# Attention products moved one slot pair earlier, with key and query loads in three pieces each

## The chip, the cores and the metric

The kernel runs on one core of a Trainium2 chip. The metric is the device time of one execution in microseconds (us). The core's engines work side by side, each through its own list of instructions in order: TensorE (PE; its weight loads are shown apart as PEld), VectorE (DVE), ScalarE (ACT), GpSimd (POOL) and SyncE (SP). POOL and SP, and at two places ACT, also issue DMA transfers, which run on 16 shared DMA engines. An engine that has to wait for a semaphore holds up everything behind it in its list.

## What is computed

Attention with a threshold, then a two-layer feed-forward stage. Batch 8, 8 heads, 576 positions, head size 64; the feed-forward stage has 4608 tokens, width 512 and inner width 2048.

```python
def _attn_ref(q, k, v, tau) -> np.ndarray:
    scale = 1.0 / np.sqrt(q.shape[-1])
    scores = scale * np.matmul(q, k.transpose(0, 1, 3, 2))
    thresh = np.max(scores, axis=-1, keepdims=True) - tau
    scores = np.where(scores >= thresh, scores, -1000000000.0)
    scores = scores - np.max(scores, axis=-1, keepdims=True)
    attn = np.exp(scores)
    attn = attn / (np.sum(attn, axis=-1, keepdims=True) + 1e-09)
    return np.matmul(attn, v).astype(np.float32)

def _moe_ref(x, w_in, w_out) -> np.ndarray:
    h = x @ w_in
    relu6 = np.clip(h + 3.0, 0.0, 6.0)
    g = h * relu6 / 6.0
    return (g @ w_out).astype(np.float32)
```

The attention output of all heads, laid side by side, is `x`.

## The kernel before

The schedule is written out by hand (`manual_schedule`), as a list of 144 **slots**, 18 for each batch. A slot is 128 query rows of one pair of heads (a slot of type `t = 4` holds the last 64 rows of two pairs). Within a batch, slots 0 to 3 hold the first 256 queries of head pairs 0 and 1, slots 4 to 7 those of pairs 2 and 3, slots 8 and 9 the last 64 queries of all, slots 10 to 17 queries 256 to 511 in the same order. In this text "slot 6 of a batch" counts from the batch's first slot, and "slot 24" alone counts from the start.

What a slot goes through, and on which engine:

- **Scores** (PE, line 216). `burst(n + 2)`, at the end of every even slot n, computes the scores of slots n + 2 and n + 3 in float32, straight into PSUM. In its middle stands a relay, an empty instruction on POOL (line 205), for which the last matmuls wait; it stands behind POOL's normalising in that slot.
- **Maximum** (DVE, line 230), which also copies the scores to SBUF, and the **bias** from it (POOL, line 239).
- **Mask and exponential** (ACT, lines 244 and 249), with the row sum; its **reciprocal** (DVE, line 252).
- **Normalising** to bf16 (POOL, line 257), in the slot after.
- **Transpose** of the probabilities. For the first ten slots PE does it; for the other 134, SP issues a DMA transpose (line 268) into `pT` (or `pR` for the last 64 queries).
- **Attention product** (`av`, PE, line 286), ten matmuls for a pair of heads and a chunk of 256 queries (forty small ones for the last 64 queries). The table `products` says in which slot each stands; it reads the values `v` of the whole batch and the transposes of two slots. For pair 0 these are the chunk's first and third slot, for pair 2 its fifth and seventh (slots 4 and 6 of the first chunk, 14 and 16 of the second), so pairs 0 and 2 have their last probabilities later, measured from the product, than pairs 1 and 3.

A finished chunk gives eight items to `todo1`, the last 64 queries of two batches give four. From slot 14 on every slot takes one item, if there is one, and multiplies it with `w_in` (`mm1`, line 309 through a helper); the gate follows on ACT or DVE (lines 327, 329, 342). Finished items give parts to `todo2`; from slot 21 on each odd slot takes two of them and multiplies with `w_out` (`mm2_part`, line 309). Each output tile is scaled on DVE (line 361) and stored by SP (line 376). The items of the last 64 queries are transposed through SP (line 344, `g<-go`). Per batch there are 18 items, 18 parts and 9 products for 18 slots, so in the middle of the run every slot is full. What is left after slot 143 is worked off in the tail: first what stands in `todo1` and `todo2`, then the last attention products, then their items and parts.

A **quad** is four heads of a batch (quad 2b and 2b + 1). Its keys and queries are loaded as one tile each (`load`, line 86, tiles `nk` and `nq`, 576 KB, two buffers each) and put in order by 32x32 block transposes on DVE (`transpose_k`, line 110, in two parts of two instructions; `transpose_q`, line 96, in two parts), which are the `jobs` of given slots. The values of a batch come in eight pieces of 64 or 80 KB (line 119) into one of two buffers. All these issues stand at the end of their slot: on SP for the loads of batches 0 and 1, on POOL for the later ones and for the values and weights. DMA issues on POOL are part of its one list: the next bias and the next normalising wait behind them.

In each slot from 14 on, the order is: maximum of the next slot, reciprocal, attention product, first-product item with its gate, two second-product parts (odd slots), exponentials, masks, block transposes, normalising of the slot before, burst (even slots), output stores, DMA issues.

Of the kernel before, what the change touches and what calls it, by code (L numbers as in the profile page):

```python
# [20 lines left out]
def kernel(  # L21
# [10 lines left out]
    nc = tc.nc  # L32
# [6 lines left out]
    NSLOT = 18  # L39
# [33 lines left out]
    issues = {}  # L73
    jobs = {}

    def at(when, n, job):
        when.setdefault(n, []).append(job)
# [3 lines left out]
    def load(quad, of, t0=0, t1=T, by=nc.sync):  # L81
        b, g = divmod(quad, 2)
        if (quad, of) not in nat:
            nat[quad, of] = nat_pool.tile([P, T * D], F32, tag=("nq", "nk")[of], name=("nq", "nk")[of])
        src = (q, k)[of][b, 4 * g:4 * g + 4].rearrange("h (r t) d -> (h r) (t d)", r=R)
        by.dma_start(out=nat[quad, of][:, t0 * D:t1 * D], in_=src[:, t0 * D:t1 * D])
# [7 lines left out]
    def transpose_q(quad, t0, t1):  # L94
        rows = nat[quad, 0][:].rearrange("p (t j w) -> p t j w", j=2, w=32)
        nc.vector.transpose(out=qk_of(quad)[0][:].rearrange("p j (t w) -> p t j w", w=32)[:, t0:t1],  # L96
                            in_=rows[:, t0:t1])
# [3 lines left out]
    def transpose_k(quad, part):  # L101
        first, e = ((0, 5), (10, 4))[part]
        rows = nat[quad, 1][:].rearrange("p (t j w) -> p j t w", j=2, w=32)
        outs = qk_of(quad)[1]
        for j in range(2):
            for_u = rows[:, j, first:first + 2 * e].rearrange("p (u e) w -> p u e w", u=2)
            base = outs[:, j, :]
            o = base[:, 64 * part:64 * part + 64].rearrange("p (u w) -> p u w", u=2)
            o = bass.AP(tensor=o.tensor, offset=o.offset, ap=[list(o.ap[0]), [32, 2], [128, e], [1, 32]])
            last = nc.vector.transpose(out=o, in_=for_u)  # L110
        return last
# [3 lines left out]
    def load_v(b):  # L115
        def piece(a, g):
            t0, count = (((0, 5), (5, 5), (10, 4), (14, 4)), ((10, 4), (14, 4), (0, 5), (5, 5)))[a][g]
            c0 = 0 if a == 0 else 5 - count
            nc.gpsimd.dma_start(  # L119
                out=vsb[b % 2][32 * g:32 * g + 32].rearrange("p (hp a) c -> p a hp c", a=2)[  # L120
                    :, a, :, c0 * D:(c0 + count) * D],
                in_=v[b].rearrange("(hp a) (r t) d -> a r hp (t d)", a=2, t=T)[a][:, :, t0 * D:(t0 + count) * D])

        return [lambda a=a, g=g: piece(a, g) for g in range(4) for a in range(2)]
# [9 lines left out]
    def load_w_in(i):  # L134
        f0 = 512 * i
        nc.gpsimd.dma_start(out=w_in_sb[:, :, f0:f0 + 512],
                            in_=moe_w_in.rearrange("(ki p) f -> p ki f", p=P)[:, :, f0:f0 + 512])
# [252 lines left out]
    products = {}  # L390
    for b in range(B):
        n0 = b * NSLOT
        for hp in range(NPAIR):
            at(products, n0 + (6 if b == 0 else 8) + 2 * hp, (b, hp, 0))
            at(products, n0 + 18 + 2 * hp, (b, hp, 1))
        at(products, n0 + (14 if b == 0 else 16), (b, None, None))

    def multiply(n):
        copies = []
# [14 lines left out]
    for quad in range(2, 2 * B):  # L414
        b, g = divmod(quad, 2)
        n0 = (b - 1) * NSLOT
        when = (((1, 4), (7, 9))[g] if b == 1 else ((-1, 5), (7, 9))[g])
        for n, of in zip(when, (1, 0)):
            at(issues, n0 + n, lambda quad=quad, of=of: load(quad, of, by=nc.sync if quad < 4 else nc.gpsimd))
        when = (((4, 8, 10, 22), (12, 14, 18, 24)) if b == 1 else ((8, 10, 12, 20), (14, 16, 18, 22)))[g]  # L420
        for n, job in zip(when, (lambda quad=quad: transpose_k(quad, 0), lambda quad=quad: transpose_k(quad, 1),
                                 lambda quad=quad: transpose_q(quad, 0, 8), lambda quad=quad: transpose_q(quad, 8, T))):
            at(jobs, n0 + n, job)
# [4 lines left out]
    def v_pieces(b, slots):  # L428
        pieces = []

        def piece(i):
            if not pieces:
                pieces.extend(load_v(b))
            pieces[i]()

        for i, n in enumerate(slots):
            at(issues, n, lambda i=i: piece(i))

    v_pieces(0, (-1, -1, -1, -1, 0, 0, 0, 0))
    for b in range(1, B):  # L440
        v_pieces(b, (13, 14, 15, 16, 17, 18, 19, 20) if b == 1 else [(b - 1) * NSLOT + n for n in range(8, 24, 2)])
    for i, n in enumerate((0, 2, 2, 3)):
        at(issues, n, lambda i=i: load_w_in(i))
    for i, n in enumerate((4, 6, 8, 10)):
        at(issues, n, lambda i=i: load_w_out(i))
# [218 lines left out]
```

## Time and profile before

| what | value |
|---|---|
| device time, median of the runs | 501.76 us (lowest 500.86) |
| profiled execution: device time | 501.7 us |
| profiled execution: span on the core | 499.9 us |
| DVE scores maximum, L230 | 288 at 750 ns |
| ACT exponential, L249 | 288 at 671 ns |
| POOL normalising, L257 | 288 at 745 ns |
| POOL issue of a key or query load, L86 | 24 at 588 to 596 ns |
| key load, POOL issue to landing, 576 KB | 4.9 us (median) |
| query load, the same | 5.1 us |
| value piece, 80 KB / 64 KB | 4.3 / 3.4 us |
| DMA transpose of probabilities, issue to landing | 4.5 us |
| all DMA | 79.98 MB, 192770 packets |

Durations, idle times and landings come from one profiled execution; the device time contains the span and 1.8 us around it. In a row of a group or of the timeline, the shape to the right of the arrow is what is read, the number after "x" the count, and the bracket at the end tells how long the engine stood idle before and whose work ended that. In the rows of the stretches, the numbers in round brackets are counts of instructions.

### The profile page before, as it was taken

What the parts mean: (1) busy time and instruction counts of PE and PEld (TensorE: products, weight loads), DVE (VectorE), ACT (ScalarE), POOL (GpSimd) and SP (SyncE); (2) the same over time, 40 slices, a digit from 0 to 9 for tenths busy, and PEclk for the clock granted to TensorE, in tenths of its full rate; (3) what the DMA queues carried; (4) which work ended last, traced back from release to release, by engine and by line L of the source; (5) the groups of instructions that cost most, each with busy time, mean ns of one, the idle gap of its engine ahead of it and who ended that gap; (6) DMA issues with size and microseconds to landing.
All of it is one profiled execution on the core that took longest, in us unless ns stands there. A gap on an engine that the chain in (4) does not pass through costs nothing.

```text
span 499.9 us, 17390 instructions
## 1 busy us (share of the span) xinstructions
PE 484.7 (97%) x6797; PEld 359.5 (72%) x6802; DVE 445.8 (89%) x1154; ACT 441.6 (88%) x949; POOL 294.1 (59%) x537
## 2 busy tenths in 40 slices
PE   8888998999999999999999999999999999999996
PEld 7766765777777776777777776777777776777474
DVE  6999986999999999999999999999999999887243
ACT  3999997999999999999999999999999999999231
POOL 3786784666666666666666666766666565554000
PEclk9999998999999999999999999999999999999999
DMA  7999998997999887997999997998999878766421
GB/s 207 150 252 178 148 181 141 180 163 117 178 178 217 130 186 149 227 158 151 156 209 181 152 168 146 220 176 147 160 187 207 151 129 130 134 123 134 92 65 42
DMA packets 192770, 79.98 MB, mean 160 GB/s; under 512 B 171184, under 2 KB 183984, under 8 KB 192688
## 3 DMA queue, kind: packets, MB, share of 16 engines
q1 hardware_dynamic: 175456, 55.34, 65.0%
q0 software_dynamic: 16896, 23.07, 23.9%
q8 instruction: 53, 0.87, 0.7%
q10 hardware_dynamic: 336, 0.46, 0.3%
q14 instruction: 29, 0.24, 0.2%
HBM read 36.70 MB, written 9.44 MB: 92 GB/s over the span
## 4 chain that ended last, share of the span: by engine, by line
PE 82%; DVE 7%; issue 1%; ACT 1%; DMA 0%; SPq 0%; DVEq 0%
PE ps L309 48%; PE ps L216 27%; PE ps L286 7%; DVE s L230 4%; DVE g L342 1%; ACT r L327 1%; DVE osb L361 1%; DMA out_dram<-osb 0%; DVE kT L110 0%; DVE r L329 0%; DVE xT L294 0%; DVE pR L279 0%; SPq L376 0%; DVE qT L96 0%; DVE rinv L252 0%
## 5 line engine op out<-in xcount | busy, mean ns | idle before, releaser
L230 DVE TENSOR_SCALAR_CACHE_REDUCE s<-ps 128x576 f32<-128x576 f32 x288 | 205.0, 750 | 17.9 <-PE ps L216 15.2
L257 POOL TENSOR_SCALAR pn<-s,rinv 128x576 bf16<-128x576 f32 x288 | 210.8, 745 | 14.9 <-issue 1.3
L244 ACT ACTIVATE s<-s,bias 128x576 f32<-128x576 f32 x288 | 205.7, 762 | 8.3 <-POOL bias L239 8.3
L249 ACT ACTIVATE s<-s 128x576 f32<-128x576 f32 x288 | 192.3, 671 | 0.0
L216 PE MATMUL ps<-kT,qT 32*128 32x128 f32 (+3 forms) x2560 | 168.6, 418 | 6.5 <-DVE s L230 4.0
L216 PEld LDWEIGHTS ps<-kT,qT 32*128 32x128 f32 (+1 forms) x2560 | 125.1, 175 | 50.9 <-DVE s L230 11.5
L309 PE MATMUL ps<-xT,w_in_sb 128*64 128x256 bf16 (+1 forms) x1936 | 133.4, 275 | 0.5 <-DVE xT L294 0.5
L309 PE MATMUL ps<-w_out_sb,g 128*64 128x512 bf16 (+1 forms) x1020 | 130.8, 379 | 0.2
L309 PEld LDWEIGHTS <-w_in_sb 128*64 128x64 bf16 (+1 forms) x1936 | 106.0, 109 | 10.9 <-issue 3.3
L239 POOL TENSOR_SCALAR bias<-m 128x2 f32<-128x2 f32 (+1 forms) x147 | 27.6, 188 | 140.1 <-DVE rinv L252 125.9
L342 DVE SCALAR_TENSOR_TENSOR g<-r,ps 128x512 bf16<-128x512 f32 x128 | 87.4, 684 | 12.2 <-ACT r L327 8.5
L309 PEld LDWEIGHTS <-g 128*64 128x64 bf16 (+1 forms) x1024 | 61.6, 109 | 47.9 <-issue 0.2
L327 ACT ACTIVATE r<-ps,three 128x512 f32<-128x512 f32 x81 | 55.2, 686 | 22.8 <-PE ps L309 21.8
L249 ACT ACTIVATION_READ_ACCUMULATOR s<-s 128x1 f32 x288 | 54.6, 190 | 0.0
L286 PEld LDWEIGHTS <-v 128*64 128x64 bf16 x960 | 41.4, 111 | 15.8 <-issue 3.8
L286 PE MATMUL ps<-pT,v 128*64 128x256 bf16 x640 | 45.4, 273 | 1.3 <-DVE s L230 1.2
L329 DVE TENSOR_SCALAR r<-ps 128x512 f32<-128x512 f32 x63 | 43.3, 688 | 0.7 <-PE ps L309 0.4
L119 POOL DMA_DIRECT2D v<-in_v_dram x64 | 36.9, 578 | 10.1 <-DVE kT L110 4.7
L361 DVE TENSOR_SCALAR osb<-ps 128x512 f32<-128x512 f32 x32 | 21.9, 684 | 9.0 <-DMA out_dram<-osb 6.3
L110 DVE STREAM_TRANSPOSE kT<-nk 128x320 f32<-128x320 f32 (+1 forms) x64 | 26.3, 452 | 0.8 <-DMA nk<-in_k_dram 0.8
L294 DVE CAST xT<-ps 128x256 bf16<-128x256 f32 x64 | 26.0, 406 | 0.4
L96 DVE STREAM_TRANSPOSE qT<-nq 128x640 f32<-128x640 f32 (+2 forms) x33 | 24.6, 749 | 1.5 <-DMA nq<-in_q_dram 1.5
(35 smaller groups left out, 170.8 us busy)
## 6 DMA issues: line engine op xcount, KB each, us to landing
out_dram<-osb SPq DMA_DIRECT2D x140, 64.0 KB, 2.6
nk<-in_k_dram POOLq DMA_DIRECT2D x12, 576.0 KB, 4.9
nq<-in_q_dram POOLq DMA_DIRECT2D x12, 576.0 KB, 5.1
v<-in_v_dram POOLq DMA_DIRECT2D x32, 80.0 KB, 4.3
v<-in_v_dram POOLq DMA_DIRECT2D x32, 64.0 KB, 3.4
w_in_sb<-in_moe_w_in_dram POOLq DMA_DIRECT2D x4, 512.0 KB, 7.7
w_out_sb<-in_moe_w_out_dram POOLq DMA_DIRECT2D x4, 512.0 KB, 9.1
pT<-pn SPq DMA_TRANSPOSE x120, 4.5
```

Of the source, the lines that this page charges most:

```text
L119: nc.gpsimd.dma_start(out=vsb[b % 2][32 * g:32 * g + 32].rearrange("p (hp a) c -> p a hp c", a=2)[:, a, :, c0 * D:(c0 + count) * D], in_=v ...
L216: mm = nc.tensor.matmul(ps_flat[rows, c0:c0 + w], qT[c:c + 32, j, q0:q0 + rows.stop - rows.start], kT[c:c + 32, j, k0:k0 + w], start=(j == ...
L230: nc.vector.tensor_scalar(out=sl.s[:, i, :], in0=ps_flat[:, c0:c0 + S], scalar1=1.0, scalar2=None, op0=Alu.mult, op1=Alu.max, accum_out=sl ...
L239: nc.gpsimd.tensor_scalar(out=sl.bias[:, of], in0=sl.m[:, of], scalar1=-scale, scalar2=tau, op0=Alu.mult, op1=Alu.add)
L244: nc.scalar.activation(out=s, in_=s, func=Act.Prelu, bias=sl.bias[:, i:i + 1], scale=scale, alpha=REJECT)
L249: nc.scalar.activation(out=s, in_=s, func=Act.Exp, accum_out=sl.rsum[:, i:i + 1])
L257: nc.gpsimd.tensor_scalar(out=pn[:, i, :], in0=sl.s[:, i, :], scalar1=sl.rinv[:, i:i + 1], scalar2=1.0, op0=Alu.mult, op1=Alu.mult)
L286: nc.tensor.matmul(pb[a * 64:(a + 1) * 64, :], vsb[b % 2][:, 2 * hp + a, u * D:(u + 1) * D], pT[:, block, cols], start=(c == 0), stop=(c = ...
L309: nc.tensor.matmul(out[c:c + w], lhsT[:, c:c + w], rhs, start=start, stop=stop)
L327: nc.scalar.activation(out=r, in_=hps, func=Act.Relu, bias=three[:])
L329: nc.vector.tensor_scalar(out=r, in0=hps, scalar1=3.0, scalar2=0.0, op0=Alu.add, op1=Alu.max)
L342: nc.vector.scalar_tensor_tensor(out=out, in0=r, scalar=6.0, in1=hps, op0=Alu.min, op1=Alu.mult)
```

## The change

Four things move in the schedule; no arithmetic changes.

1. The attention products of batches 1 to 7 stand two slots sooner, in slots 6 to 12 (first chunk), 14 (last 64 queries) and 16 to 22 (second chunk) of the batch. Batch 0 had its first chunk and its last 64 queries there already; its second chunk moves too. With them the items and parts that come out of them move.
2. Key and query loads of batches 2 to 7 are issued in three pieces of six query or key blocks (192 KB) each, in slots 0 to 5, 7, 9, 11, 13, 15 and 17 of the batch before (batch 2's first six in slots 3 to 8 of batch 1). Batch 1's loads stay whole and on SP.
3. The value pieces move two slots sooner (batch 1's two slots later, to slots 15 to 22), and the fourth load of `w_in` from slot 3 to slot 4.
4. The last block transpose of quad 3's queries moves from slot 24 to slot 23.

```diff
         for hp in range(NPAIR):
-            at(products, n0 + (6 if b == 0 else 8) + 2 * hp, (b, hp, 0))
-            at(products, n0 + 18 + 2 * hp, (b, hp, 1))
-        at(products, n0 + (14 if b == 0 else 16), (b, None, None))
+            at(products, n0 + 6 + 2 * hp, (b, hp, 0))
+            at(products, n0 + 16 + 2 * hp, (b, hp, 1))
+        at(products, n0 + 14, (b, None, None))
...
-        when = (((1, 4), (7, 9))[g] if b == 1 else ((-1, 5), (7, 9))[g])
-        for n, of in zip(when, (1, 0)):
-            at(issues, n0 + n, lambda quad=quad, of=of: load(quad, of, by=nc.sync if quad < 4 else nc.gpsimd))
-        when = (((4, 8, 10, 22), (12, 14, 18, 24)) if b == 1 else ((8, 10, 12, 20), (14, 16, 18, 22)))[g]
+        if b == 1:
+            for n, of in zip(((1, 4), (7, 9))[g], (1, 0)):
+                at(issues, n, lambda quad=quad, of=of: load(quad, of))
+        else:
+            when = ((((3, 4, 5), (6, 7, 8)), ((9, 10, 11), (13, 15, 17))) if b == 2 else
+                    (((0, 1, 2), (3, 4, 5)), ((7, 9, 11), (13, 15, 17))))[g]
+            for of in (1, 0):
+                for i, n in enumerate(when[1 - of]):
+                    at(issues, n0 + n, lambda quad=quad, of=of, i=i: load(quad, of, 6 * i, 6 * i + 6, by=nc.gpsimd))
+        when = (((4, 8, 10, 22), (12, 14, 18, 23)) if b == 1 else ((8, 10, 12, 20), (14, 16, 18, 22)))[g]
...
-        v_pieces(b, (13, 14, 15, 16, 17, 18, 19, 20) if b == 1 else [(b - 1) * NSLOT + n for n in range(8, 24, 2)])
-    for i, n in enumerate((0, 2, 2, 3)):
+        v_pieces(b, (15, 16, 17, 18, 19, 20, 21, 22) if b == 1 else [(b - 1) * NSLOT + n for n in range(6, 22, 2)])
+    for i, n in enumerate((0, 2, 2, 4)):
         at(issues, n, lambda i=i: load_w_in(i))
```

Here `n0` is the first slot of the batch in the first hunk, and of the batch before in the second. Keys are `of = 1`, queries `of = 0`.

## The prediction

> **What bounds the kernel now.** I read the page's busy shares first, then the same shares stage by stage, then the timeline where the stages were not alike.
>
> ```profile
> PE 484.7 (97%) x6797; PEld 359.5 (72%) x6802; DVE 445.8 (89%) x1154; ACT 441.6 (88%) x949; POOL 294.1 (59%) x537
> ...
> PEclk9999998999999999999999999999999999999999
> ```
>
> PE is busy for 97% of the span, so at most 15.2 us of idle PE can be won, plus what the one dip of its clock costs. Busy time by stretch (columns: length; PE, PEld, DVE, ACT, POOL busy; PE clock; DMA share):
>
> ```profile
> 77.68:88.00 10.32, 8.32 (x126) 5.98 (x122) 6.20 (x20) 6.92 (x17) 5.67 (x10) 0.83 0.67 145
> 88.00:112.96 24.96, 23.23 (x362) 18.27 (x360) 24.45 (x66) 24.13 (x53) 15.97 (x30) 1.00 0.97 172
> 112.96:454.88 341.92, 341.04 (x5135) 253.40 (x5133) 329.72 (x850) 326.09 (x706) 215.56 (x391) 1.00 0.96 165
> 454.88:499.90 45.02, 40.98 (x282) 26.01 (x285) 17.62 (x31) 16.48 (x29) 3.09 (x5) 1.00 0.38 82
> ```
>
> From 113 to 455 us PE has no gap; a pair of slots takes 6.30 us, and DVE (96%) and ACT (95%) follow close behind. In the tail PE works through what the slots left over. Between 77.68 and 88.00 one pair of slots took 10.32 us. The timeline (start, length, engine, line) tells why:
>
> ```profile
> 77.93 0.43 PE L216 MATMUL ps<-kT,qT 32*64 32x128 f32 x2
> 79.46 0.83 DVE L96 STREAM_TRANSPOSE qT<-nq 128x640 f32<-128x640 f32 x1
> 80.35 3.40 PE L216 MATMUL ps<-kT,qT 32*64 32x128 f32 x62 [2.00 <-DVE qT L96]
> ```
>
> The scores issued in slot 24 (queries 512 to 575 of batch 1) need the transpose of quad 3's last ten query blocks, which is a job of that same slot. PE waited 2.00 us, and then its clock was down (0.83 over the stretch, 1.75 us lost).
>
> **The tail.** Following the lists through all slots: before, slots 22, 23 and 24 find no first-product item and odd slots 29, 31, 49 no second-product part; after, only slot 22, and 29 and 47. So the tail is left with 7 first-product items instead of 9, 4 waiting parts instead of 6, and 3 attention products instead of 4. From the tail's rows, 40 matmuls for five items took 4.56 us (0.91 an item), 14 parts 12.25 us (0.87 a part), four products 2.37 us (0.59). Sum: 1.82 + 1.75 + 0.59 = 4.2 us off the path, since PE sets the tail. The last softmax has cover: slot 143's transpose landed at 463.2, its product ran at 477.6, and 4 us less still leaves 10.
>
> **The slots that take this work.** Work that leaves the tail is only won where PE idled.
>
> Slot 16 gains a product (0.55 us, the spacing of ten L286 matmuls). Its transposed probabilities landed at 54.53 and PE could start it at 53.9, so it also waits some 0.3. The burst behind it took 2.81 us against 2.23 undisturbed, because it waited for DVE; that 0.58 is cover. Net +0.3 (0 to 0.9).
>
> Slot 20 now takes the product that needs slot 16's probabilities. Their normalising ended at 62.35 and the fastest transpose in the trace takes 3.2 us, so they are there at 65.6 to 66.6 when PE asks at 65.0. Wait 0.6 to 1.6; the burst behind it has 0.4 of the same cover (2.64 against 2.23). Net +0.7 (0.2 to 1.2).
>
> Slots 23 to 26: the two pairs took 5.29 + 10.32 = 15.6 us. With the late transpose in slot 23 (DVE ends it near 78.7, before the fuller PE reaches that burst) they should take 2 x 6.30 with all their items: -3.0. But slot 24 now takes batch 1's first product, which reads all eight value pieces. The last piece moved from slot 20 to 22, behind a key piece in the same POOL queue: normalising ends there at 74.8, two issues of 0.6 follow, and a value piece lands 3.4 to 4.3 us after its issue, so near 79, while PE, one item later than before, asks at 77.9. Wait 1.1 (0 to 3, beyond 2 with the clock loss of 1.75 again). Net -1.9 (-3.0 to +1.7).
>
> Slot 31's two parts: the pairs of slots 29 to 34, without those parts, took 18.7 us against 18.9 for full ones, so they cost +0.2. Slot 23's transpose (0.83) is the same work on DVE one slot sooner. The third input-weight load one pair later is needed about 30 us on: 0.
>
> By the Trainium skill ("TensorE: Matmul & The Clock Gate", the section on HAM oscillation) only PE gaps of more than about 3.4 us cost clock. The 2.00 us gap here was followed by 0.83 of the clock. By the page the gap would be worth 2.0 us, by the row 3.75.
>
> **The steady batches.** The products read probabilities that POOL normalises and SP's transpose brings. For a product of head pair 2, first chunk (batch 4):
>
> ```profile
> 256.02 1.47 POOL L257 TENSOR_SCALAR pn<-s,rinv 128x576 bf16<-128x576 f32 x2
> 257.43 0.59 POOL L86 DMA_DIRECT2D nk<-in_k_dram  x1
> 259.22 1.67 SPq L268 DMA_TRANSPOSE pT<-pn  x1
> 262.82 0.71 PE L286 MATMUL ps<-pT,v 128*64 128x256 bf16 x10
> 269.12 0.71 PE L286 MATMUL ps<-pT,v 128*64 128x256 bf16 x10
> ```
>
> Normalising ends at 257.5, and the product runs at 269.1; moved one pair sooner it takes the place at 262.8, 5.3 us after it. Head pair 0 has 5.0 to 5.3, pairs 1 and 3 and the rest over 8. So 28 products (pairs 0 and 2, two chunks, batches 1 to 7) stand if normalising to landing takes under about 5.2. In the trace that took 8.2 in the middle case for the one shown, 5.6 for pair 2's second chunk, 3.3 and 4.1 for pair 0. What stretches it is the 576 KB load: issued within 0.1 us of the normalising's end in both pair 2 cases. In batch 7, which has no such loads, it is clean. Transposes of pT over the whole run, then from 427 us on:
>
> ```profile
> DMA to landing us min/median/max: 3.2/4.5/9.1
> ...
> DMA to landing us min/median/max: 3.2/3.2/4.9
> ```
>
> Each piece is 192 KB. A whole load added 2.4 to 3.7 us, a third of it about 1; value pieces (64 or 80 KB) beside a transpose gave 3.7 to 4.8. I therefore take 4.2 to 4.5 for the critical ones, with one in six or so over 5.2. Two things also leave the way of pair 2: SP's queue holds the transpose of g and the output stores in front of it (it was issued 1.7 us late above), and both move one pair sooner. 28 x 1/6 x 0.3 us is 1.4, taken as +1.5 (0 to 8, the upper end being 0.3 us on every one). PE has no slack, so each such wait counts in full.
>
> POOL issues 48 more loads at 0.59 us: 28 us, 4 to 5 per batch of 56.7, on an engine busy for 63% there. In even slots they stand behind the normalising and the burst's relay, before POOL's idle 1.6 to 2.2 us. In odd slots the bias, normalising and relay queue behind them, and ACT and PE behind these; pairs with such a load before (slots 5, 7, 9, 17) took 6.30 like the others, so 0. Were that cover gone, some 30 of them at 0.3 us would be 9 us. DVE's block transposes find their pieces: the closest is quad 1's query piece of slot 15 for slot 18, two and a half slots or 8 us against a landing of 5.1 for a whole load.
>
> The Trainium skill ("DMA: Bandwidth & Descriptors", rules for kernel authors) speaks against the pieces: coalesce, since each DMA has about 2 us fixed cost. If that stood on the path, 48 extra loads would be an estimated 96 us. Here loads of 64 KB land in 3.4 us and those of 576 KB in 4.9, and nothing waits that closely, so the rule does not decide.
>
> **Sum.** Tail -4.2, early slots +0.3 +0.7 -1.9 +0.2 = -0.7, steady +1.5: -3.4. The profiled execution took 501.7 us (span 499.9 and 1.8 around it), as the median of 501.76 does. That gives 498.3.
>
> **Rivals.** *The waits hardly come*: the steady term is 0, slot 24 finds its values, slot 20 its probabilities: -4.2 -2.6, so 495. For it: batch 7's clean landings. Against: slot 20's arithmetic.
>
> *The products become late in every batch* and PE waits for SP's transpose. Place: head pairs 0 and 2. Price: 28 times the excess over 5.2 us. It undoes the gain from a mean of 0.17 us on (4.9 / 28); at 0.3, 8.4 us come in place of 1.5: 505. With the old latencies, 8.2 and 5.6 for pair 2, it would be 14 products times 0.4 to 2.9, up to 23 us net: 520. For it: the DMA share of 0.96 leaves little room. Against: the bytes beside a critical transpose fall to a third.
>
> *The early region gives the gain back*: slot 24 waits over 2 us for values and the clock drops again, about +3.6: 502. It also covers the change failing to do what it says, with the tail bound by something other than PE; then only the early terms stay, near 501.
>
> **How the numbers follow.** Forecast 0.5, waits hardly come 0.2, late products 0.2, gain given back early 0.1. The range 494.5 to 504.5 leaves out the far ends of the first and third, some 0.2. Two per cent, about what a measurement tells from no change, is 10 us: under 491.7 needs more than all terms at their best (0.03), over 511.8 a mean wait of 0.6 us at every critical product (0.06).
>
> **What would show it.** In the profile after: no 2.00 us wait on the query transpose and no clock dip near 81 us; a tail some 4 us shorter; pair starts still 6.30 apart; waits at L286 on DMA, small, at pairs 0 and 2. Wrong it would be if L286 waits on pT add up to over 5 us, if PE waits on POOL, or if a gap of 2 us stands before slot 24's product.

## The result, and the profile after

The changed kernel takes 504.66 us (median of 14 runs, 501.8 to 508.22) against 501.9 us for the kernel before on the same chip: 1.0064 times, 95% interval 1.0041 to 1.0086, so 2.8 us longer. The profiled execution took 508.2 us with a span of 506.4 us; it is the slowest of the 14, which matters when its stages are read. I look at the shares first, as before.

The page's busy shares and the row of PE's clock, kernel after:

```profile
PE 485.0 (96%) x6822; PEld 359.3 (71%) x6826; DVE 448.4 (89%) x1156; ACT 440.7 (87%) x947; POOL 319.4 (63%) x585
...
PEclk9999989999999999999999999999999999999999
```

PE is busy as long as before (485.0 us against 484.7) and idles 21.4 us instead of 15.2: 6.2 of the 6.5 us that the span grew. POOL's busy time rose by 25 us, and nothing in the rest of this text waits for it. The row of the clock still has a dip, one slice earlier; a second one is rounded away in it and shows in the stretches below.

To see which stage lost time I cut both spans at the starts of the score bursts of the same slots (worked out from the starts of the L216 matmuls), so that each piece holds the same slots (us):

| piece | before | after | difference |
|---|---|---|---|
| start to the burst for slot 14 | 43.25 | 43.75 | +0.5 |
| from there to the burst for slot 36 | 69.95 | 77.5 | +7.6 |
| from there to the burst for slot 142 | 334.0 | 336.4 | +2.45 |
| the rest, with the tail | 52.75 | 48.75 | -4.0 |

The tail gave its 4 us, and the early slots took nearly twice that. Stretches of the kernel after (columns as in the prediction):

```profile
65.00:69.80 4.80, 1.70 (x26) 1.26 (x24) 3.54 (x11) 4.80 (x13) 3.33 (x8) 1.00 1.27 142
69.80:73.30 3.50, 3.50 (x40) 2.92 (x38) 1.61 (x3) 1.11 (x2) 1.90 (x3) 0.54 0.75 139
80.00:86.90 6.90, 4.95 (x73) 3.61 (x67) 4.74 (x13) 6.83 (x16) 5.77 (x11) 1.00 0.92 192
86.90:90.30 3.40, 3.40 (x53) 2.13 (x55) 2.04 (x4) 1.13 (x2) 0.80 (x2) 0.53 1.12 111
...
121.30:461.40 340.10, 337.46 (x5087) 250.14 (x5088) 326.89 (x839) 320.93 (x695) 232.47 (x424) 1.00 0.91 165
```

Between 65 and 69.8 us PE worked 1.70 of 4.80 us, and the stretch behind it ran at 0.54 of the clock; between 80 and 86.9 it idled 1.95 us, and again the stretch behind ran at half speed. Two waits, then, and two dips, where the kernel before had one of each. From 121 to 461 us PE idles 2.6 us in 340.

The timeline at the first of them (start, length, engine, line, what is written and read; the bracket is idle time and its releaser):

```profile
62.39 1.47 POOL L257 TENSOR_SCALAR pn<-s,rinv 128x576 bf16<-128x576 f32 x2
...
63.80 0.57 POOL L119 DMA_DIRECT2D v<-in_v_dram  x1
...
65.83 0.58 POOL L119 DMA_DIRECT2D v<-in_v_dram  x1
...
69.52 0.81 PE L286 MATMUL ps<-pT,v 128*64 128x256 bf16 x10 [3.10 <-DMA pT<-pn]
70.11 1.92 PE L309 MATMUL ps<-xT,w_in_sb 128*64 128x256 bf16 x16
```

This is slot 20's product. Slot 16's probabilities are normalised by 63.9; their transpose is issued at once. Two value pieces, those of slots 17 and 18, are issued at 63.80 and 65.83 and travel at the same time. The transpose of `pT` in this window, and then those of the whole run:

```profile
DMA to landing us min/median/max: 5.6/5.6/5.6
...
DMA to landing us min/median/max: 3.2/4.1/6.4
```

It took 5.6 us, where the prediction had reckoned 3.2 to 4.2. The same transpose in the kernel before, with what POOL issued around it:

```profile
62.54 0.60 POOL L86 DMA_DIRECT2D nk<-in_k_dram  x1
63.14 0.55 POOL L119 DMA_DIRECT2D v<-in_v_dram  x1
...
65.13 0.57 POOL L119 DMA_DIRECT2D v<-in_v_dram  x1
```

```profile
DMA to landing us min/median/max: 7.3/7.3/7.3
```

There it took 7.3 us, with a whole key load and two value pieces beside it, the pieces of the same two slots. The change took the key load away and left two pieces there; it made this transpose faster. Nobody had waited for it, because the product stood in slot 22; moved to slot 20, it waits. The second wait, in slot 24:

```profile
81.23 0.61 POOL L86 DMA_DIRECT2D nk<-in_k_dram  x1
...
81.84 0.55 POOL L119 DMA_DIRECT2D v<-in_v_dram  x1
...
83.35 0.84 DVE L96 STREAM_TRANSPOSE qT<-nq 128x640 f32<-128x640 f32 x1
83.54 0.27 PE L286 MATMUL ps<-pT,v 128*64 128x256 bf16 x1
85.77 0.73 PE L286 MATMUL ps<-pT,v 128*64 128x256 bf16 x9 [1.95 <-DMA v<-in_v_dram]
```

The first matmul of batch 1's first product runs, the other nine wait for a value piece: the last one, issued behind a key piece. The block transpose of the queries, which was the wait before, is done meanwhile and costs nothing here.

The steady batches, head pair 2 of batch 4, at the place shown before:

```profile
265.57 1.46 POOL L257 TENSOR_SCALAR pn<-s,rinv 128x576 bf16<-128x576 f32 x2
...
272.48 0.74 PE L286 MATMUL ps<-pT,v 128*64 128x256 bf16 x10
```

The product stands 5.45 us behind the normalising (forecast: 5.3) and doesn't wait. PE's largest waits for DMA in the whole run (total us, times, longest):

```profile
PE ps L286 <- DMA pT<-pn: 5.8, 4, 3.1
...
PE ps L286 <- DMA v<-in_v_dram: 2.0, 1, 2.0
```

Of the 5.8 us on the transposes, 3.1 are slot 20's. In the steady batches the largest is 1.24 us (slot 56, pair 2 of batch 2).

### The profile page after: what moved, and what is told of

It is laid out like the page before. It is cut to its first block, busy times and chain, and to the rows that moved or that the text cites. A ratio compares the mean times of both kernels' runs of the same rounds, so it can differ in the third digit from the quotient of the medians.

```text
span 506.4 us, 17501 instructions
## 1 busy us (share of the span) xinstructions
PE 485.0 (96%) x6822; PEld 359.3 (71%) x6826; DVE 448.4 (89%) x1156; ACT 440.7 (87%) x947; POOL 319.4 (63%) x585
## 4 chain that ended last, share of the span: by engine, by line
PE 75%; DVE 7%; DMA 5%; issue 2%; POOL 2%; ACT 1%; SPq 0%; POOLq 0%; DVEq 0%
PE ps L309 43%; PE ps L216 24%; PE ps L286 7%; DMA pT<-pn 4%; DVE s L230 3%; POOL pn L257 1%; DVE g L342 1%; DMA v<-in_v_dram 1%; ACT r L327 1%; DVE kT L110 1%; DVE osb L361 1%; DVE r L329 0%; DMA out_dram<-osb 0%; POOL bias L239 0%; DVE xT L294 0%
## 5 line engine op out<-in xcount | busy, mean ns | idle before, releaser
L216 PE MATMUL ps<-kT,qT 32*128 32x128 f32 (+3 forms) x2560 | 167.7, 421 | 5.0 <-DVE s L230 4.0
L216 PEld LDWEIGHTS ps<-kT,qT 32*128 32x128 f32 (+1 forms) x2560 | 124.9, 177 | 49.4 <-DVE s L230 10.5
L286 PEld LDWEIGHTS <-v 128*64 128x64 bf16 x960 | 41.0, 111 | 25.7 <-issue 6.5
L286 PE MATMUL ps<-pT,v 128*64 128x256 bf16 x640 | 46.0, 274 | 9.6 <-DMA pT<-pn 5.8
```

Of the source, the lines that this page charges most:

```text
L216: mm = nc.tensor.matmul(ps_flat[rows, c0:c0 + w], qT[c:c + 32, j, q0:q0 + rows.stop - rows.start], kT[c:c + 32, j, k0:k0 + w], start=(j == ...
L286: nc.tensor.matmul(pb[a * 64:(a + 1) * 64, :], vsb[b % 2][:, 2 * hp + a, u * D:(u + 1) * D], pT[:, block, cols], start=(c == 0), stop=(c = ...
```

## The experiments

The theory is that the loss sits in two early slots and comes from two parts of the change which the rest of it doesn't need: batch 0's second chunk moved sooner (slot 20 waits for a transpose), and batch 1's value pieces moved later (slot 24 waits for one). The rivals are that the 48 more loads cost POOL or the DMA engines time everywhere, that the products are late in every batch, and that the block transpose in slot 23 does harm. Edits are to the changed kernel unless said otherwise. PE's waits below are from the rows of each run's profile. The value pieces of batches 2 to 7 and the `w_in` load were not moved back by themselves; what they cost is inside every version below that has the sooner products.

**The value pieces back where they were.**

```diff
-        v_pieces(b, (15, 16, 17, 18, 19, 20, 21, 22) if b == 1 else [(b - 1) * NSLOT + n for n in range(6, 22, 2)])
+        v_pieces(b, (13, 14, 15, 16, 17, 18, 19, 20) if b == 1 else [(b - 1) * NSLOT + n for n in range(6, 22, 2)])
```

> The changed kernel with batch 1's value pieces back in slots 13 to 20 instead of 15 to 22; all else as changed. Theory 1 (the early waits cost the time: slot 20 waited 3.10 us for slot 16's transpose, slot 24 waited 1.95 us for the last value piece, and each was followed by 3.4 us at half clock): the 1.95 us wait and its clock dip go, 1.95 + 1.7 = 3.6 us less than the changed kernel, near 501; slot 20's wait stays or grows by some tenths, since two value pieces come nearer to it. Theory 2 (the fuller slots 23 and 24 are bound by DVE and ACT, and the wait only takes slack): no change, 504 to 505. Theory 3 (the loss is spread over the batches by POOL's 48 more issues and small waits): no change.

Measured 503.71 us, 1.0031 of before (1.0008 to 1.0054). Slot 24's wait for values is gone. Slot 20's stays (2.87 us, transpose 5.4 us in flight), since pieces are still issued in slots 17 and 18, at 63.84 and 65.87; a dip follows it. That is 1.0 us less than the changed kernel, where 3.6 were expected; between the two profiles, each one execution, it is 3.9.

**Batch 0's second chunk back**, to slots 18, 20, 22 and 22 (the last of the four had stood in 24 before).

```diff
-            at(products, n0 + 16 + 2 * hp, (b, hp, 1))
+            at(products, 18 + (0, 2, 4, 4)[hp] if b == 0 else n0 + 16 + 2 * hp, (b, hp, 1))
```

> The changed kernel with batch 0's second-chunk products in slots 18, 20, 22, 22 instead of 16, 18, 20, 22, so that the chunk is still complete in slot 22. Theory 1: the waits of 0.72 us in slot 16 and 3.10 us in slot 20 go, and the first clock dip (1.7 us) with them: up to 5.5 us less than the changed kernel, near 499 to 500; slot 24's wait for values stays and may grow, since PE comes there sooner. Theory 2: at most 1 us. Theory 3: none.

Measured 501.07 us, 0.9986 (0.9968 to 1.0005): 3.6 us less than the changed kernel (up to 5.5 expected). PE's waits in this run:

```profile
PE ps L286 <- DMA v<-in_v_dram: 1.8, 1, 1.8
PE ps L286 <- DMA pT<-pn: 1.5, 3, 0.6
```

Slot 20's wait has gone, slot 24's has not. So the two are separate, and slot 20's is the larger.

**Both of them**, in two runs apart, the second of five rounds:

> Both of the above. Theory 1: both waits and both dips go, 8 to 9 us less than the changed kernel, 495 to 497, which is below both kernels. Theory 2: near 503. Theory 3: near 504.

> The version with both early waits removed once more, with more rounds, on the same chip as the one above. Theory 1: 498.5 to 499.2, a ratio of 0.992 to 0.996 to the kernel before.

Measured 498.85 us, 0.994 (0.9921 to 0.9959), and 499.2 us, 0.9939 (0.9916 to 0.9962). This is faster than both kernels, but by less than the 495 to 497 that the theory gave. The timeline of PE in the first of them, where slots 22 to 24 are:

```profile
72.27 1.26 PE L286 MATMUL ps<-pT,v 128*64 128x256 bf16 x20
...
78.62 0.71 PE L286 MATMUL ps<-pT,v 128*64 128x256 bf16 x10
...
80.13 2.71 PE L216 MATMUL ps<-kT,qT 32*64 32x128 f32 x64
```

Two products stand side by side in slot 22 (20 matmuls), slot 24's product follows without a wait, and so does its burst. No dip shows. With batch 0's second chunk back, the place of the value pieces is worth 2.2 us (501.07 against 498.85). The pieces of the span: slots 14 to 36 took 69.2 us (before 69.95), slots 36 to 142 335.05 (before 333.97), the rest 48.74 (before 52.74). Its -0.75 in the early slots equals the prediction's early term of -0.7 by chance: slots 24 and 26 gained 2.2 us, slots 28 to 34 lost 0.9 and slot 22 lost 0.5, and no product stands in slot 16.

**The block transpose alone**, on the kernel before:

```diff
-        when = (((4, 8, 10, 22), (12, 14, 18, 24)) if b == 1 else ((8, 10, 12, 20), (14, 16, 18, 22)))[g]
+        when = (((4, 8, 10, 22), (12, 14, 18, 23)) if b == 1 else ((8, 10, 12, 20), (14, 16, 18, 22)))[g]
```

> The kernel before with the last block transpose of quad 3's queries in slot 23 instead of 24, and nothing else. Theory 1: the 2.00 us wait and the clock dip after it go (3.7 us), of which DVE and ACT, which stand close behind PE there, take back up to 1.5: 498 to 500. If the clock dip does not hang on this wait: 500.

Measured 499.78 us, 0.9971 (0.9951 to 0.9992). The 2.00 us wait and the dip went; the slots 14 to 36 took 67.3 us, 2.65 less. So item 4 does no harm: by itself it gives 2 us. It also prices the rest. Beside it, the version with both parts undone is only 0.6 to 0.9 us faster: -4.0 in the tail, +1.9 in slots 14 to 36 (69.2 against 67.3), +1.1 in the steady batches (335.05 against 333.96).

**The loads in pieces alone**, on the kernel before, with item 2's loads and nothing else:

```diff
-        when = (((1, 4), (7, 9))[g] if b == 1 else ((-1, 5), (7, 9))[g])
-        for n, of in zip(when, (1, 0)):
-            at(issues, n0 + n, lambda quad=quad, of=of: load(quad, of, by=nc.sync if quad < 4 else nc.gpsimd))
+        if b == 1:
...
+                for i, n in enumerate(when[1 - of]):
+                    at(issues, n0 + n, lambda quad=quad, of=of, i=i: load(quad, of, 6 * i, 6 * i + 6, by=nc.gpsimd))
```

> The kernel before with the key and query loads of batches 2 to 7 in three pieces at the changed kernel's slots; products, values and the late transpose as before. It shows what the 48 more issues on POOL (28 us of POOL) cost alone. Theory 1: nothing, 501.5 to 502.5. Theory 3: up to 9 us more than before, spread over the batches as pairs longer than 6.30 us.

Measured 502.35 us, 1.0002 (0.998 to 1.0023). Slots 36 to 142 took 333.96 us, to 0.01 us what they took with 24 whole loads. 48 more issues on POOL cost nothing that shows; the interval leaves room for 1 us.

**Whole loads with the sooner products**: the changed kernel with the lines of item 2 taken back.

```diff
-        if b == 1:
-            for n, of in zip(((1, 4), (7, 9))[g], (1, 0)):
-                at(issues, n, lambda quad=quad, of=of: load(quad, of))
-        else:
...
+        when = (((1, 4), (7, 9))[g] if b == 1 else ((-1, 5), (7, 9))[g])
+        for n, of in zip(when, (1, 0)):
+            at(issues, n0 + n, lambda quad=quad, of=of: load(quad, of, by=nc.sync if quad < 4 else nc.gpsimd))
```

> The changed kernel with the loads whole again (576 KB, in the slots of the kernel before). If the pieces are what makes the sooner products possible, transposes of head pair 2 land late again (8.2 and 5.6 us after the normalising, against 5.3 that they have): 12 products wait 0.3 to 2.9 us, 10 to 20 us more than the changed kernel, 515 to 525. If the pieces do not matter: 504 to 505.

Measured 515.13 us, 1.0277 (1.0226 to 1.0327), 10.5 us more than with pieces. The two profiles are 6.9 us apart, and slots 36 to 142 account for all of it (343.7 against 336.4). PE's waits for the transposes, and the transposes' flights:

```profile
PE ps L286 <- DMA pT<-pn: 11.1, 8, 5.2
```

```profile
DMA to landing us min/median/max: 3.2/4.0/7.8
```

The worst flight is 7.8 us instead of 6.4, and eight products wait instead of four; the pairs of slots 28, 38, 46, 56, 64, 74, 82, 92, 100, 110 and 118 took 6.6 to 8.2 us. Slot 16's transpose, with the whole key load beside it again, took 7.7 us, and slot 20's product waited 5.2. So item 2 is what makes the sooner products possible: without it this change would have cost 13 us. It changes the size of the loads and the slots of their issue together; which of the two does it was not separated.

**Is it the wait or the clock?** PE is kept busy in slot 20 with 16 multiplications that nobody reads:

```diff
         item = todo1.pop(0) if todo1 else None
+        if n == 20:
+            warm_up(16)
         for copy in multiply(n):
```

> The changed kernel with 16 blank PE transposes (0.165 us each, 2.6 us) ahead of slot 20's product, so that PE works during the wait for slot 16's transpose. The product cannot come sooner. If the half clock after it follows from PE's idle time, the dip goes and 1.7 us with it: 502.5 to 503. If the dip has another cause: no change, 504 to 505, or a little more.

Measured 504.15 us, 1.0063 (1.0039 to 1.0087). The timeline of PE in its profile:

```profile
65.86 2.40 PE L152 MATMUL ps<-identf 128*128 128x128 f32 x20
...
68.94 0.74 PE L286 MATMUL ps<-pT,v 128*64 128x256 bf16 x10 [0.68 <-DMA pT<-pn]
69.51 1.04 PE L309 MATMUL ps<-xT,w_in_sb 128*64 128x256 bf16 x16
```

The 16 matmuls of `mm1` behind the product took 1.04 us instead of 1.92, so the clock was whole, and the pair of slot 20 took 8.18 us instead of 9.78. Of these 1.6 us the product's sooner start is 0.7, since the transpose landed after 4.9 us in this run; 0.9 is the clock, and another 0.7 of the clock's share lies in the next pair (5.43 us against 6.14). But the median of the times fell by 0.5 us only. Slot 24's wait of 2.0 us is still there, and by the mean clocks 5 of these 10 runs lie below 0.999, against 8 of the changed kernel's 14; only runs as low as 0.993 are rarer (1 against 4). So this one profile fits idle time as the cause of the dip, and the times do not price it.

**The value pieces far ahead**, so that none lies beside slot 16's transpose: slots 5 to 12 for batch 1. Batch 0's second chunk stays sooner in the first run and goes back in the second.

```diff
-        v_pieces(b, (15, 16, 17, 18, 19, 20, 21, 22) if b == 1 else [(b - 1) * NSLOT + n for n in range(6, 22, 2)])
+        v_pieces(b, (5, 6, 7, 8, 9, 10, 11, 12) if b == 1 else [(b - 1) * NSLOT + n for n in range(6, 22, 2)])
```

> The changed kernel with batch 1's value pieces in slots 5 to 12, beside the w_out loads, instead of 15 to 22; products where the change puts them. It tells why slot 16's transpose took 5.6 us. If the two value pieces beside it (slots 16 and 17) stretched it: it lands 3.2 to 3.5 us after its issue, slot 20's wait falls from 3.10 to 0.5 to 1.0 us, slot 24's value wait is gone, and the time is 497 to 499. If the transpose is slow for another reason: slot 20 still waits 2.5 us or more, near 503 as with the values at 13 to 20.

> The same values in slots 5 to 12, and batch 0's second-chunk products in slots 18, 20, 22, 22. If early values are free: at or up to 1 us under the 498.85 of the version with values at 13 to 20. If they cost something where they now stand (they delay the PE transposes' copies or the w_out loads): above it.

Measured 500.96 us, 0.9988 (0.9969 to 1.0008), where 497 to 499 was expected, and 499.01 us, 0.9936 (0.9911 to 0.9961). The transpose in the first run, and PE at slot 20's product:

```profile
DMA to landing us min/median/max: 3.2/3.2/3.2
```

```profile
68.70 0.74 PE L286 MATMUL ps<-pT,v 128*64 128x256 bf16 x10 [0.69 <-DMA pT<-pn]
```

With no value piece beside it the same transpose takes 3.2 us instead of 5.6, and the wait is 0.69 us instead of 3.10, with no dip. That 0.69 is what the prediction had reckoned for this slot (0.6 to 1.6). The pieces are not all of it: in the second run the same transpose took 4.5 us, without a piece or a load in flight, where the version above had 5.2. What held it up there is open. The second run, with the product back, is 2 us faster (500.96 against 499.01). In the profiles 0.9 us of the difference lies in slots 14 to 36, where the pair of slot 16 took 6.32 us with a product in it (4.73 without one in the version above); 1.6 us lies ahead of slot 14, where the two have the same work in the same order, so how much of the 2 us is the product's stays open. The second run (four timed runs) equals the version above, where the pieces are in slots 13 to 20; with the product later, slots 5 to 12 and 13 to 20 are alike.

**The block transpose once more**, in the version that is faster than both: back in slot 24 in the first run, as the diff shows; in slot 22 in the second (22 in the place of 24).

```diff
-        when = (((4, 8, 10, 22), (12, 14, 18, 23)) if b == 1 else ((8, 10, 12, 20), (14, 16, 18, 22)))[g]
+        when = (((4, 8, 10, 22), (12, 14, 18, 24)) if b == 1 else ((8, 10, 12, 20), (14, 16, 18, 22)))[g]
```

> The version with both early waits removed (batch 0's products in 18, 20, 22, 22, values at 13 to 20), with the late block transpose back in slot 24. What the transpose in slot 23 is worth inside the new schedule: if PE, which is fuller there by two items, hides most of the wait, under 1 us more, 499 to 500; if it is worth the same as alone (2.2 us), 501.

> The version with both early waits removed (batch 0's products in 18, 20, 22, 22, values at 13 to 20), with the late block transpose in slot 22, which has no item and so no gate on DVE, instead of 23. In slot 23 PE still waited 0.5 us for it. If that wait is the last that the early slots lose to it: 0.3 to 0.8 us under the version with slot 23. If DVE, which then has two block transposes in slot 22, delays the burst behind it instead: the same or up to 1 us more.

Measured 502.82 us, 1.0017 (0.9995 to 1.0039), and 499.14 us, 0.9936 (0.9912 to 0.9961). Slot 24 in the first of them:

```profile
80.08 0.43 PE L216 MATMUL ps<-kT,qT 32*64 32x128 f32 x2
...
82.12 0.83 DVE L96 STREAM_TRANSPOSE qT<-nq 128x640 f32<-128x640 f32 x1
83.01 1.87 PE L216 MATMUL ps<-kT,qT 32*64 32x128 f32 x26 [2.50 <-DVE qT L96]
```

The wait of before is back, larger (2.50 us against 2.00), with its dip: 4.0 us more than in slot 23, nearly twice what the move was worth in the old schedule (2.2). That a fuller PE would hide the transpose was wrong: DVE comes to it 1.6 us after PE has begun to wait, against 1.1 before. That this is because DVE's slot is fuller too is argued, not shown. Slot 22 gives nothing over slot 23: once nobody waits, sooner is no better.

## Why the prediction was wrong

The forecast was 498.3 us and a range to 504.5; it came to 504.66. Point by point:

**The tail** was right: -4.0 in the profile of every version with sooner products, for -4.2.

**The steady term** was right in sign and size: +2.45 us in the changed kernel's profile, 0.8 to 2.4 in the five with no wait of a microsecond or more in slots 20 to 24 and the transpose in slot 23 or 22 (334.79 to 336.38 against 333.97), for +1.5. The waits are at head pair 2, as forecast, but fewer and longer than the sum had them: the pair of slot 56 took 1.4 us more and that of slot 128 0.7 (its wait is put down to DVE in this profile), where four or five waits of 0.3 were reckoned. So the sum of them agreed partly by luck.

**POOL's 48 more issues at nothing** held (1.0002 with them alone). The Trainium skill's advice to coalesce ("DMA: Bandwidth & Descriptors", rules for kernel authors), put at an estimated 96 us if it stood on the path, did not hold here: with the sooner products the pieces are 10.5 us faster than whole loads, with the old ones equal.

**The early slots** are the step that failed: forecast at -0.7, they came to +7.6 in the profile. By pairs of slots, each from the start of one burst to the start of the next ("slot 16" is slots 15 and 16 and the burst ahead of them):

| pair | before | after | forecast of the difference | measured |
|---|---|---|---|---|
| slot 16 | 4.74 | 6.08 | +0.3 (0 to 0.9) | +1.3 |
| slot 18 | 5.86 | 5.45 | 0 | -0.4 |
| slot 20 | 6.03 | 9.78 | +0.7 (0.2 to 1.2) | +3.75 |
| slot 22 | 5.84 | 6.14 | 0 | +0.3 |
| slots 24 and 26 | 15.60 | 17.08 | -1.9 (-3.0 to +1.7) | +1.5 |
| slots 28 to 34 | 24.97 | 26.07 | +0.2 | +1.1 |

Two misses are about equal, slot 20 by 3.0 us and slots 24 and 26 by 3.4.

*Slot 20*. The step that failed is the flight of slot 16's transpose: the prediction took the fastest transpose of the trace (3.2 us, to 4.2) for one that its own trace showed at 7.3 us, beside a key load and two value pieces. The change took away the load only, and the flight came to 5.6 us and the wait to 3.10 instead of 0.6 to 1.6. The prediction also had the row "value pieces (64 or 80 KB) beside a transpose gave 3.7 to 4.8" and used it for the steady batches, not here. The landings and the end of normalising that it read for slots 12, 16 and 143 stand 0.25 us earlier than in the trace (54.53 for 54.78, 62.35 for 62.60, 463.2 for 463.45), which moves no term by more than that.

*Slots 24 and 26* went as written down, but in other sizes: the last value piece, behind a key piece in POOL's queue. The sooner block transpose was worth 2.6 us by itself (-3.0 in the sum); the wait for values was 1.95 us, inside its bounds (0 to 3) but not the 1.1 taken; and it was followed by a dip (1.7 us), where the clock loss was set to begin beyond 2 us. Some 0.5 us is left over.

*The clock* has a part in both. The prediction counted 1.75 us for the dip that goes, and none for a dip that comes, although its own row had 0.83 of the clock behind a gap of 2.00 us. Slots 20 and 24 both got a gap and a dip. Without the two dips (1.7 us each) and the one of before, the early region would have lost 5.9 us in this profile.

*Slot 16* and the pair behind it together took 0.9 us more, the upper end of the forecast of +0.3 (0 to 0.9). The burst's wait for DVE, which was to be cover, did go (2.22 us instead of 2.81); that burst is counted in the row of slot 18. The product's own wait was 0.72 us and not 0.3: the trace before had the transpose landing at 54.78 and PE free at 53.92, which is 0.9, and even the prediction's 54.53 gives 0.6.

*Slots 28 to 34* lost 1.1 us in this profile and 0.9 with both parts undone, for +0.2; what takes the time there was not followed up.

Of the rivals, "the early region gives the gain back" is the one that came, with its mechanism (slot 24 waits for values, the clock drops again) and with slot 20, which it did not name; so its 502 was too low. Two of the prediction's own signs of being wrong came as well: waits at L286 on pT add up to 5.8 us (mark: 5), and a gap of 1.95 us stands before slot 24's product (mark: 2). "The products become late in every batch" did not come with pieces; with whole loads it did, at 515.1 us, between its two prices of 505 and 520.

The size of the loss depends on the execution. The profile of the changed kernel holds both dips and is 6.5 us longer; its median run is 2.8 us longer. Each timed run also tells its mean clock: the changed kernel's runs without a dip (clock 0.999 or more, 6 runs) have a median of 503.2 us, those of before (12 of the 31 runs timed beside the first four experiments) 500.6, those with a mean of 0.993 took 506.8 to 508.2. So without any dip the change costs some 2.6 us, and dips add to that in some runs. That is nearly the whole of the 2.8 us: in the median it is the waits that lost the time, since the kernel before has dips in many of its runs too. The dips make up much of what the profile shows beyond that.

## What to carry to other kernels

When a change makes someone wait for a transfer that nobody waited for, take that transfer's own time in the trace before, with what travels beside it, and ask which of these neighbours the change takes away; the fastest of its kind is the wrong price (here 3.2 us for one that took 7.3 before and 5.6 after). Sooner work for a full engine is won only where its inputs are there, so check the first batch by itself, where loads are late and pieces crowd: there this schedule lost more than the tail gave, and putting two things back, the products of batch 0's second chunk and batch 1's value pieces, made it 0.994 times the time before. A list that is moved whole ("all batches") should be split where the start differs from the steady part.

## What was not expected of the hardware

Gaps of PE near 2 us are sometimes followed by half the clock for 3.41 us, which costs about 1.7 us, and sometimes not. In the profiles: dips behind gaps of 2.00 (before, and with the pieces alone), 3.10 and 1.95 (after), 2.87 (value pieces back) and 2.50 us (block transpose back in slot 24); none behind 1.77 us (batch 0's chunk back) and none behind 2.0 in the run with the busy wait. The Trainium skill ("TensorE: Matmul & The Clock Gate", HAM oscillation) puts the bound at about 3.4 us; these six dips came behind shorter gaps, so the measurement decides, and a gap of 2 us must be reckoned at 2.0 to 3.7 us. The whole-load version's gap of 5.2 us was followed by 6.83 us at half speed.

The traces show what goes with a dip. In all fourteen profiles the clock changes only at whole multiples of 3.413 us after it first comes to full speed (in the changed kernel after 19, 20, 24 and 25 of them). With the span cut into these windows, and the end of each run left out, where PE has no more work: of the windows at full clock, each of the seven in which PE idled 1.70 us or more was followed by half the clock, and none of the others (1.69 us at most) was. The two nearest to the border, with the pieces alone (a dip follows) and with the busy wait (none follows); the second column is PE's busy time:

```profile
78.59:82.00 3.41, 1.71 (x20) 0.90 (x16) 3.41 (x11) 3.41 (x9) 2.55 (x6) 1.00 0.87 193
...
81.96:85.37 3.41, 1.75 (x37) 1.55 (x45) 1.96 (x8) 3.41 (x8) 2.48 (x5) 1.00 0.96 198
```

So a gap of 2.0 us brings a dip when 1.7 us of it fall into one window: it lay inside one in the kernel before, and was cut in two in the run with the busy wait (81.61 to 83.62, with a border at 81.96). Where the windows lie against the program differs from run to run. If it is by chance, a gap of 2.0 us would meet this in about 0.6 of the runs (an estimate: (3.41 - 1.70 + 0.30) / 3.41); 19 of those 31 runs of the kernel before have a mean clock below 0.999. This is read from the traces, and no run varied it.

Two small plain loads held up a DMA transpose as much as a large one did in the kernel before: 5.6 us in flight beside two value pieces of 64 or 80 KB, 3.2 us without them (4.5 us in another version without them), where by the prediction's rows a whole load of 576 KB had added 2.4 to 3.7 us.
